# A down-projection in Strassen form with seven quadrant products, its shared sums carried on by copying PSUM banks

## The chip, the cores and the metric

One Trainium2 chip, one core. The metric is the device time of one launch in microseconds (us). The kernel before takes 472.49 us (median of 4 runs, 472.24 to 472.75). Batches are numbered from 0 to 7. A "half" is half of one batch's sequence, 512 positions. The engines are called by the profile's names: PE multiplies matrices, PEld loads its weights, DVE and ACT work on elements, POOL issues the k, v, q and weight loads, SP issues the transposing transfers. PSUM is the memory in which PE adds up its products; a bank is one tile of it, here 128x512 in fp32. The "granted clock" is PE's clock in the profile, as a share of full speed.

## The reference

Linear attention with a fixed projection, then a token-and-channel mixer, over 8 batches of 1024 positions:

```python
k_proj = einsum('ks,bhsd->bhkd', E, k);  v_proj = einsum('ks,bhsd->bhkd', F, v)   # 64 of 1024
attn   = softmax(q @ k_proj.T / 8);      x = heads_side_by_side(attn @ v_proj)    # (8, 1024, 512)
u  = x + (relu(x.T @ w_tok1) @ w_tok2).T          # token mixing
out = u + relu(u @ w_ch1) @ w_ch2                 # channel mixing, 512 -> 1536 -> 512
```

The last product, `relu(...) @ w_ch2`, is the down-projection that the change rewrites.

## The kernel before

Everything runs in bf16 with fp32 sums in PSUM. While the "back" of batch b (channel mixing: `up` and `down`) runs, the "front" of batch b+1 (projections, attention, token mixing) is cut into small units that are put between its blocks, and the k, v and q of batch b+2 are loaded. Parts of the code:

```python
def q_transpose(b):                       # two transposing transfers, SBUF to SBUF, issued by SP
    for h in range(0, H, H // 2):
        tc.keep_in_program_order(nc.sync.dma_start_transpose(out=qT[:, h:h+H//2]..., in_=q_sb[:, h:h+H//2]...))

def ch2(i, ss, part):                     # 4 of the 12 products of one 128x512 output tile
    if part == 0:
        st["o"] = psC.tile([P, DM], F32, tag="c", name="o2_ps")
    for cc in range(part * 4, part * 4 + 4):
        nc.tensor.matmul(o2_ps, st["gT", i][:, cc, ss*P:(ss+1)*P], wc2_sb[:, cc, :], ...)
    if part == CC // 4 - 1:
        nc.vector.tensor_add(out=o_sb, in0=o2_ps, in1=u_sb[:, si, :]); stores.append(...)

def load_ahead(b, cc):                    # the loads wait for Relu tile cc of the batch's first half
    passed = nc.gpsimd.tensor_copy(out=gate, in_=first_tile()[0:1, cc, 0:1])
    with tc.issue_after(passed.ins):
        load_kv(b + 2, 2); load_q(b + 2, 2)

units = front_units(b + 1)
units.append(lambda b=b: q_transpose(b + 2))        # last unit of the batch
for n, block in enumerate(blocks):
    block()
    if b > 0 and n == 5:
        load_ahead(b, 5)
    # [...] then as many units as are due
```

"The u transpose" below is SP's other transfer, which turns u into the uT that the up-projection reads. A scheduler orders the instructions of each engine when the kernel is built, and the profile shows the engines starting them in that order: on DVE in batch 0, below, an addition that was ready stands behind an operation that waits.

The softmax here doesn't subtract the row's maximum and nothing guards it: scores larger than these inputs give would overflow.

Of the kernel before, what the change touches and what calls it, by code (L numbers as in the profile page):

```python
# [8 lines left out]
F32 = mybir.dt.float32  # L9
BF16 = mybir.dt.bfloat16  # L10
# [5 lines left out]
def kernel(  # L16
# [13 lines left out]
    nc = tc.nc  # L30
    P = 128

    B, H, S, D = q.shape
    KP = E.shape[0]
    DM = H * D
# [3 lines left out]
    NSI = S // P  # L39
    NJ = NSI // 2  # L40
    TC = DT // P
    DMC = DM // P
    CC = DC // P
    HP = H // 2
    S2 = S // 2
# [1 line left out]
    scale = 1.0 / (D ** 0.5)  # L47

    const = ctx.enter_context(tc.tile_pool(name="const", bufs=1))
    kv_pool = ctx.enter_context(tc.tile_pool(name="kv", bufs=2))  # L50
    small = ctx.enter_context(tc.tile_pool(name="small", bufs=2))
    attn_pool = ctx.enter_context(tc.tile_pool(name="attn", bufs=4))
    mix_pool = ctx.enter_context(tc.tile_pool(name="mix", bufs=2))
    gT_pool = ctx.enter_context(tc.tile_pool(name="gT", bufs=2))
    out_pool = ctx.enter_context(tc.tile_pool(name="outp", bufs=5))
    psC = ctx.enter_context(tc.tile_pool(name="psC", bufs=3, space=bass.MemoryType.PSUM))
    psA = ctx.enter_context(tc.tile_pool(name="psA", bufs=2, space=bass.MemoryType.PSUM))
    psS = ctx.enter_context(tc.tile_pool(name="psS", bufs=1, space=bass.MemoryType.PSUM))
# [11 lines left out]
    def load_kv(b, parts):  # L70
        k_sb, v_sb, q_sb = [
            kv_pool.tile([P, H, NSI, D], BF16, tag=name, name=name) for name in ("k_sb", "v_sb", "q_sb")
        ]
        qT = mix_pool.tile([P, H, NJ, P], BF16, tag="qT", name="qT")
        loaded[b] = (k_sb, v_sb, q_sb, qT)
        hn = H // parts
        for h in range(0, H, hn):
            for t, src in ((k_sb, k), (v_sb, v)):
                nc.gpsimd.dma_start(
                    out=t[:, h : h + hn],  # L80
                    in_=src[b, h : h + hn].rearrange("h (p si) d -> p h si d", p=P),
                )

    def load_q(b, parts):
        hn = H // parts
        for h in range(0, H, hn):
            nc.gpsimd.dma_start(
                out=loaded[b][2][:, h : h + hn],
                in_=q[b, h : h + hn].rearrange("h (p si) d -> p h si d", p=P),
            )  # L90

    def q_transpose(b):
        q_sb, qT = loaded[b][2:]
        for h in range(0, H, H // 2):
            tc.keep_in_program_order(
                nc.sync.dma_start_transpose(
                    out=qT[:, h : h + H // 2].rearrange("p h j s -> p (h j) s"),
                    in_=q_sb[:, h : h + H // 2].rearrange("p h si d -> p (h si d)"),
                )
            )  # L100

    load_kv(0, HP)
    load_q(0, HP)

# [5 lines left out]
    for c in range(0, DC, DC // 4):  # L110
        nc.gpsimd.dma_start(
            out=wc1_sb[:, :, c : c + DC // 4],
            in_=moe_w_ch1.rearrange("(dc p) c -> p dc c", p=P)[:, :, c : c + DC // 4],
        )
    load_kv(1, 2)
    load_q(1, 2)
    wc2_sb = const.tile([P, CC, DM], BF16, name="wc2_sb")
    for c in range(0, CC, CC // 4):
        nc.gpsimd.dma_start(
            out=wc2_sb[:, c : c + CC // 4],  # L120
            in_=moe_w_ch2.rearrange("(cc p) d -> p cc d", p=P)[:, c : c + CC // 4],
# [15 lines left out]
    for src, dst in ((E_sb, ET_sb), (F_sb, FT_sb)):  # L137
# [2 lines left out]
            nc.tensor.transpose(e_ps[:, si, :], src[:, si:S:NSI], ident[:KP, :KP])  # L140
        nc.vector.tensor_copy(out=dst, in_=e_ps)

    uTs = {}
    us = {}

    def front_units(b):

        k_sb, v_sb, q_sb, qT = loaded.pop(b)
        vb = vbs[b % 2]
        x_sb = mix_pool.tile([P, NSI, DM], BF16, tag="x_sb", name="x_sb")  # L150
        u_sb = mix_pool.tile([P, NSI, DM], BF16, tag="u_sb", name="u_sb")
        hT_sb = mix_pool.tile([P, TC, DM], BF16, tag="hT_sb", name="hT_sb")
        uT = [
            mix_pool.tile([P, NJ, DMC, P], BF16, tag=f"uT{i}", name=f"uT{i}") for i in range(2)
        ]
# [1 line left out]
        st = {}  # L157

        def q_transpose_pe(hp):
            t_ps = psC.tile([P, 2, NJ, P], BF16, tag="c", name="t_ps")  # L160
            for h in range(2):
                for j in range(NJ):
                    nc.tensor.transpose(  # L163
                        t_ps[:, h, j, :],
                        q_sb[:, 2 * hp + h, 2 * j : 2 * j + 2, :].rearrange("p s d -> p (s d)"),
                        ident,
                    )
            nc.scalar.copy(out=qT[:, 2 * hp : 2 * hp + 2], in_=t_ps)  # L168
# [117 lines left out]
        if b == 0:  # L286
            for hp in range(HP):
                kv_proj(2 * hp, 2)
                k_transpose(2 * hp, 2)
            q_transpose_pe(0)  # L290
            q_transpose_pe(1)
            scores(0)
            q_transpose_pe(2)
            scores(1)
            attend(0)
# [31 lines left out]
        units = [kv_proj, k_transpose]  # L327
# [11 lines left out]
    stores = []  # L339

    def flush(n):

        for dst, o_sb in stores[:n]:
            nc.scalar.dma_start(out=dst, in_=o_sb)
        del stores[:n]

    out_v = out.rearrange("b (p si) d -> b p si d", p=P)

    def back_blocks(b):

        u_sb, uT = us.pop(b), uTs.pop(b)
        st = {}

        def ch1(i, cc):
            g_ps = psC.tile([P, S2], F32, tag="c", name="g_ps")
            for dc in range(DMC):
                nc.tensor.matmul(  # L357
                    g_ps, wc1_sb[:, dc, cc * P : (cc + 1) * P], uT[i][:, :, dc, :],
                    start=(dc == 0), stop=(dc == DMC - 1),
                )  # L360
            nc.scalar.activation(out=st["gT", i][:, cc, :], in_=g_ps, func=ACT.Relu)  # L361

        def ch2(i, ss, part):
            if part == 0:
                st["o"] = psC.tile([P, DM], F32, tag="c", name="o2_ps")
            o2_ps = st["o"]
            for cc in range(part * 4, part * 4 + 4):
                nc.tensor.matmul(  # L368
                    o2_ps, st["gT", i][:, cc, ss * P : (ss + 1) * P], wc2_sb[:, cc, :],
                    start=(cc == 0), stop=(cc == CC - 1),  # L370
                )
            if part == CC // 4 - 1:
                si = i * NJ + ss
                o_sb = out_pool.tile([P, DM], F32, tag="o_sb", name="o_sb")
                nc.vector.tensor_add(out=o_sb, in0=o2_ps, in1=u_sb[:, si, :])  # L375
                stores.append((out_v[b, :, si, :], o_sb))

        def half(i):
            st["gT", i] = gT_pool.tile([P, CC, S2], BF16, tag="gT", name="gT")

        up, down = [], []
        for i in range(2):
            up.append([lambda i=i: (half(i), ch1(i, 0))])
            up[i] += [lambda i=i, cc=cc: ch1(i, cc) for cc in range(1, CC)]
            down.append(
                [lambda i=i, ss=ss, p=p: ch2(i, ss, p) for ss in range(NJ) for p in range(CC // 4)]
            )
        if b == 0:
            blocks = up[0] + up[1] + down[0] + down[1]
        else:  # L390
            blocks = up[0] + down[0] + up[1] + down[1]
        return blocks, lambda: st["gT", 0]
# [3 lines left out]
    def load_ahead(b, cc):  # L396

        if b + 2 < B:
            passed = nc.gpsimd.tensor_copy(out=gate, in_=first_tile()[0:1, cc, 0:1])  # L399
            with tc.issue_after(passed.ins):  # L400
                load_kv(b + 2, 2)
                load_q(b + 2, 2)

    rest = front_units(0)
    for b in range(B):
        blocks, first_tile = back_blocks(b)
        if b == 0:
            for n, block in enumerate(blocks[:16]):
                block()
                if rest:  # L410
                    rest.pop(0)()
            load_ahead(0, 0)
            blocks = blocks[16:]
        n0, n1 = (0, len(blocks) - 4) if b == 0 else (2, len(blocks) - 4)
        units = front_units(b + 1) if b + 1 < B else []
        if b + 2 < B:
            units.append(lambda b=b: q_transpose(b + 2))
        done = 0
        for n, block in enumerate(blocks):
            made = len(stores)  # L420
            block()
            if b > 0 and n == 5:
                load_ahead(b, 5)
            want = max(0, n + 1 - n0) * len(units) // (n1 - n0)
            while done < min(want, len(units)):
                units[done]()
                done += 1
            flush(made)
# [29 lines left out]
```

## Time and profile before

| stage | from, to (us) | length |
|---|---|---|
| batch 0, with its own front | 0 to 98.6 | 98.6 |
| batches 1 to 6, each | for example 153.1 to 207.6 | 54.5 |
| batch 7, nothing beside it | 425.6 to 471.2 | 45.6 |

A stage ends, to 0.2 us, where the next batch's first up-projection matmul starts. First the page's busy times of the kernel before, as a share of the span:

```profile
PE 451.5 (96%) x2588; PEld 221.8 (47%) x2624; DVE 175.0 (37%) x345; ACT 165.0 (35%) x259; POOL 50.1 (11%) x78
```

Then its table by stretches. After the stretch and its length come the busy us of each engine, the clock granted to PE, the share of the DMA engines and GB/s:

```profile
0.00:98.60 98.60, 84.71 (x653) 50.10 (x658) 41.60 (x102) 37.15 (x55) 26.95 (x43) 1.00 0.95 165
153.10:207.60 54.50, 54.24 (x293) 25.48 (x296) 21.16 (x39) 18.93 (x30) 4.64 (x7) 1.00 0.70 136
425.60:471.20 45.60, 41.37 (x191) 18.60 (x190) 6.23 (x9) 14.27 (x24) 0.00 (x0) 1.00 0.18 63
```

In a middle batch PE is busy 54.24 of 54.50 us at full clock. It waits for nothing, so a microsecond of PE issue saved should be a microsecond gained, and a new wait of PE should cost its whole length.

### The profile page before, as it was taken

How to read it: one execution, taken by the hardware profiler on the slowest of the kernel's cores; microseconds unless marked ns; L12 is line 12 of the kernel's file. 1: busy time of each engine (PE TensorE's matmuls, PEld its weight loads, DVE VectorE, ACT ScalarE, POOL GpSimd, SP SyncE). 2: the span in 40 equal slices, each digit the busy share in tenths (PEclk: the TensorE clock that was granted, in tenths of full speed). 3: DMA queues.
4: the chain of work that ended last, by engine and by line, in shares of the span. 5: the costliest groups of instructions: out<-in, count | busy, mean ns of one | idle time of the engine just before them, and what ended most of it. 6: DMA issues, size and time to landing. Idle time of an engine off the chain costs nothing.

```text
span 471.2 us, 6248 instructions
## 1 busy us (share of the span) xinstructions
PE 451.5 (96%) x2588; PEld 221.8 (47%) x2624; DVE 175.0 (37%) x345; ACT 165.0 (35%) x259; POOL 50.1 (11%) x78
## 2 busy tenths in 40 slices
PE   2789999999999999999999999999999999999996
PEld 2567455444544444444444445443444445444442
DVE  3454026533524343423614425242524236150202
ACT  1256581026250533316151352406242162505060
POOL 8532300003000210003000030003000000000000
PEclk9999999999999999999999999999999999999999
DMA  8999993389905895279913898069942812033102
GB/s 118 208 203 207 206 206 105 84 188 164 212 1 130 162 206 131 48 170 145 222 41 90 178 165 193 1 159 155 207 106 67 176 26 90 0 90 89 68 22 89
DMA packets 93051, 60.43 MB, mean 128 GB/s; under 512 B 56160, under 2 KB 84320, under 8 KB 93024
## 3 DMA queue, kind: packets, MB, share of 16 engines
q0 software_dynamic: 29728, 29.63, 38.6%
q1 hardware_dynamic: 54080, 13.63, 16.7%
q10 hardware_dynamic: 9216, 16.78, 9.9%
q8 instruction: 20, 0.33, 0.3%
q14 instruction: 7, 0.06, 0.0%
HBM read 59.24 MB, written 16.78 MB: 161 GB/s over the span
## 4 chain that ended last, share of the span: by engine, by line
PE 93%; DMA 4%; DVE 1%; POOL 1%; issue 1%; POOLq 0%
PE g_ps L357 36%; PE o_ps L368 35%; PE u_ps L243 5%; PE h_ps L234 5%; PE o_ps L216 3%; PE kv_ps L178 3%; PE s_ps L204 2%; DMA q_sb<-in_q_dram 2%; DMA k_sb<-in_k_dram 1%; PE up_ps L271 1%; PE t_ps L163 1%; PE hp_ps L260 1%; DVE x_sb L224 1%; PE kt_ps L193 1%; PE ut_ps L281 0%
## 5 line engine op out<-in xcount | busy, mean ns | idle before, releaser
L361 ACT ACTIVATE gT<-g_ps 128x512 bf16<-128x512 f32 x192 | 114.9, 601 | 216.8 <-PE g_ps L357 194.8
L368 PE MATMUL o_ps<-wc_sb,gT 128*128 128x512 bf16 x744 | 180.7, 379 | 1.4
L357 PEld LDWEIGHTS <-wc_sb 128*128 128x128 bf16 x768 | 71.7, 98 | 84.4 <-issue 7.2
L368 PEld LDWEIGHTS <-gT 128*128 128x128 bf16 x768 | 72.5, 98 | 78.4 <-issue 2.0
L375 DVE TENSOR_TENSOR o_sb<-o_ps,u_sb 128x512 f32<-128x512 f32 x64 | 44.3, 691 | 77.3 <-PE o_ps L368 77.3
L247 DVE TENSOR_TENSOR u_sb<-u_ps,x_sb 128x512 bf16<-128x512 f32 x56 | 38.7, 691 | 91.5 <-PE u_ps L243 84.0
L224 DVE TENSOR_TENSOR x_sb<-o_ps,rdn 128x512 bf16<-128x512 f32 x64 | 44.3, 692 | 2.2
L209 ACT ACTIVATE a_sb<-s_ps 128x1024 bf16<-128x1024 f32 x32 | 33.0, 1033 | 28.2 <-PE s_ps L204 28.2
L223 DVE RECIPROCAL rdn<-o_ps 128x8 f32<-128x8 f32 x64 | 13.0, 204 | 64.5 <-PE o_ps L216 64.4
L243 PE MATMUL u_ps<-hT_sb,wt_sb 128*128 128x512 bf16 x107 | 32.2, 378 | 0.1
L183 DVE CAST kp_sb<-kv_ps 64x512 bf16<-64x512 f32 (+1 forms) x22 | 10.9, 532 | 48.0 <-PE kv_ps L179 48.0
L216 PEld LDWEIGHTS <-a_sb 128*128 128x128 bf16 x256 | 20.2, 101 | 15.9 <-DVE x_sb L224 2.7
L399 POOL COPY gate<-gT 1x1 bf16<-1x1 bf16 x6 | 1.1, 178 | 248.1 <-ACT gT L361 248.1
L234 PE MATMUL h_ps<-x_sb,wt_sb 128*128 128x512 bf16 x105 | 26.1, 379 | 0.4
L243 PEld LDWEIGHTS <-wt_sb 128*128 128x128 bf16 x112 | 16.1, 144 | 12.2 <-issue 2.6
L179 PE MATMUL kv_ps<-v_sb,FT_sb 128*64 128x512 bf16 (+1 forms) x88 | 17.4, 354 | 4.0 <-DMA v_sb<-in_v_dram 4.0
L178 PE MATMUL kv_ps<-k_sb,ET_sb 128*64 128x512 bf16 (+1 forms) x88 | 18.3, 355 | 1.9 <-DMA k_sb<-in_k_dram 1.9
L234 PEld LDWEIGHTS <-wt_sb 128*128 128x128 bf16 x112 | 10.9, 98 | 13.2
L238 ACT ACTIVATE hT_sb<-h_ps 128x512 bf16<-128x512 f32 x14 | 8.4, 598 | 24.1 <-PE h_ps L234 24.1
L216 PE MATMUL o_ps<-vb_134,a_sb 128*128 128x130 bf16 x128 | 13.7, 235 | 1.8 <-DVE x_sb L224 1.8
L178 PEld LDWEIGHTS <-ET_sb 128*64 128x64 bf16 x88 | 8.9, 129 | 12.5 <-issue 7.7
L168 ACT COPY qT<-t_ps 128x1024 bf16<-128x1024 bf16 x8 | 8.2, 1030 | 18.1 <-PE t_ps L163 18.1
(67 smaller groups left out, 356.2 us busy)
## 6 DMA issues: line engine op xcount, KB each, us to landing
out_dram<-o_sb ACTq DMA_DIRECT2D x64, 256.0 KB, 3.5
k_sb<-in_k_dram POOLq DMA_DIRECT2D x14, 512.0 KB, 9.2
v_sb<-in_v_dram POOLq DMA_DIRECT2D x14, 512.0 KB, 11.8
q_sb<-in_q_dram POOLq DMA_DIRECT2D x14, 512.0 KB, 17.5
wc_sb<-in_moe_w_ch_dram POOLq DMA_DIRECT2D x8, 384.0 KB, 16.8
k_sb<-in_k_dram POOLq DMA_DIRECT2D x4, 256.0 KB, 7.3
v_sb<-in_v_dram POOLq DMA_DIRECT2D x4, 256.0 KB, 7.9
q_sb<-in_q_dram POOLq DMA_DIRECT2D x4, 256.0 KB, 10.0
```

The source lines that it names most:

```text
L178: nc.tensor.matmul(kv_ps[0:KP], ET_sb[:, si, :], k_sb[:, hs, si, :], start=a, stop=z)
L179: nc.tensor.matmul(kv_ps[KP : 2 * KP], FT_sb[:, si, :], v_sb[:, hs, si, :], start=a, stop=z)
L209: nc.scalar.activation(out=a_sb, in_=s_ps, func=ACT.Exp, scale=scale)
L216: nc.tensor.matmul(o_ps[:, j // 2, (j % 2) * 2 * D1 : (j % 2 + 1) * 2 * D1], a_sb[:, h % 2, j * P : (j + 1) * P], vb[:, h // 2, h % 2].rea ...
L224: nc.vector.tensor_tensor(out=x_sb[:, :, h * D : (h + 1) * D].rearrange("p (n c) d -> p n c d", n=2), in0=o4[:, :, :, 0:D], in1=rdn[:, :, ...
L234: nc.tensor.matmul(h_ps, wt1_sb[:, si, t * P : (t + 1) * P], x_sb[:, si, :], start=(si == 0), stop=(si == NSI - 1),)
L243: nc.tensor.matmul(u_ps, wt2_sb[:, t, si::NSI], hT_sb[:, t, :], start=(t == 0), stop=(t == TC - 1),)
L247: nc.vector.tensor_add(out=u_sb[:, si, :], in0=u_ps, in1=x_sb[:, si, :])
L357: nc.tensor.matmul(g_ps, wc1_sb[:, dc, cc * P : (cc + 1) * P], uT[i][:, :, dc, :], start=(dc == 0), stop=(dc == DMC - 1),)
L361: nc.scalar.activation(out=st["gT", i][:, cc, :], in_=g_ps, func=ACT.Relu)
L368: nc.tensor.matmul(o2_ps, st["gT", i][:, cc, ss * P : (ss + 1) * P], wc2_sb[:, cc, :], start=(cc == 0), stop=(cc == CC - 1),)
L375: nc.vector.tensor_add(out=o_sb, in0=o2_ps, in1=u_sb[:, si, :])
```

## The change

The intent: a 2x2 block product by Strassen (in Winograd's arrangement) needs 7 products of quadrants instead of 8. Per half, the 12 chunks of the inner dimension, the 512 output columns and the 512 positions are each cut in two. 48 matmuls of 512 columns become 7 x 12 = 84 of 256 columns. The weight side has its four sums made once, the activation side four sums per half on DVE. The outputs share partial sums. The change gets these by letting PE accumulate in bank A, copying A to B on ACT, and going on accumulating in both. To make room, k, v, q, qT, x and h go from two buffers to one. The diff, cut to its core (the comments are not in the code, and the lines p1 to p4 sum up the seven products; left out are fewer output buffers, three larger ones instead of five, and another PSUM pool for the q transposes that PE makes in batch 1):

```diff
-    kv_pool = ctx.enter_context(tc.tile_pool(name="kv", bufs=2))
+    kv_pool = ctx.enter_context(tc.tile_pool(name="kv", bufs=1))
-        qT = mix_pool.tile([P, H, NJ, P], BF16, tag="qT", name="qT")
+        qT = one_pool.tile([P, H, NJ, P], BF16, tag="qT", name="qT")      # [...] x_sb, hT_sb too
+    def weight_sums():                      # T[0] = B12-B11, T[1] = B22-T[0], T[2] = B22-B12, T[3] = B21-T[1]
+        nc.vector.tensor_sub(out=T[0], in0=B12, in1=B11)                  # [...]
+        def act_sums(i, c0, c1):            # for two chunks at a time
+            nc.vector.tensor_add(out=S1, in0=A21, in1=A22)
+            nc.vector.tensor_sub(out=S2_, in0=S1, in1=A11)
+            nc.vector.tensor_sub(out=S3, in0=A11, in1=A21)
+            nc.vector.tensor_sub(out=S4, in0=A12, in1=S2_)
+        def product(bank, left, right, first, last):
+            for t in range(2):
+                for cc in range(CH):
+                    nc.tensor.matmul(bank[:, t, :], left[:, cc, t*P:(t+1)*P], right[:, cc, :],
+                        start=(first and t == 0 and cc == 0), stop=(last and cc == CH - 1), ...)
+        def fork(src, dst):
+            nc.scalar.copy(out=bank(dst), in_=st[src])
+            # p1: A  = A11 B11, fork A->B     p5: E = S1 T0 (other bank)   p6: B += S2 T1, fork B->C
+            # p2: A += A12 B21, out 11        p7: C += S3 T2, fork C->D, out 22 (with E)
+            # p3: B += S4 B22, out 12 (with E)                 p4: D += A22 T3, out 21
             load_ahead(0, 0)
+            weight_sums()
-            if b > 0 and n == 5:
-                load_ahead(b, 5)
+            if b > 0 and n == 5:
+                load_ahead(b, 2)            # the chunks now run 0, 6, 1, 7, 2, ...: chunk 2 is the fifth Relu
+        t0, t1 = (0, total - 8) if b == 0 else (4, total - 8)             # units are due by cost, up to t1
-            while done < min(want, len(units)):
+            while free and done < min(want, len(units)):
```

The stores become 32 of 512 KB instead of 64 of 256 KB.

More of the change, by code (lines that the diff above doesn't have):

```diff
@@ L53 @@
     mix_pool = ctx.enter_context(tc.tile_pool(name="mix", bufs=2))
+    one_pool = ctx.enter_context(tc.tile_pool(name="one", bufs=1))
     gT_pool = ctx.enter_context(tc.tile_pool(name="gT", bufs=2))
-    out_pool = ctx.enter_context(tc.tile_pool(name="outp", bufs=5))
+    out_pool = ctx.enter_context(tc.tile_pool(name="outp", bufs=3))
     psC = ctx.enter_context(tc.tile_pool(name="psC", bufs=3, space=bass.MemoryType.PSUM))
@@ L141 @@
         nc.vector.tensor_copy(out=dst, in_=e_ps)
+    CH, DH = CC // 2, DM // 2
+    B11, B12 = wc2_sb[:, 0:CH, 0:DH], wc2_sb[:, 0:CH, DH:DM]
+    B21, B22 = wc2_sb[:, CH:CC, 0:DH], wc2_sb[:, CH:CC, DH:DM]
+    tw_sb = const.tile([P, 4, CH, DH], BF16, name="tw_sb")
+    def weight_sums():
+        T = [tw_sb[:, n] for n in range(4)]
+        nc.vector.tensor_sub(out=T[0], in0=B12, in1=B11)
+        nc.vector.tensor_sub(out=T[1], in0=B22, in1=T[0])
+        nc.vector.tensor_sub(out=T[2], in0=B22, in1=B12)
+        nc.vector.tensor_sub(out=T[3], in0=B21, in1=T[1])
     uTs = {}
@@ L149, in front_units @@
         vb = vbs[b % 2]
-        x_sb = mix_pool.tile([P, NSI, DM], BF16, tag="x_sb", name="x_sb")
+        x_sb = one_pool.tile([P, NSI, DM], BF16, tag="x_sb", name="x_sb")
         u_sb = mix_pool.tile([P, NSI, DM], BF16, tag="u_sb", name="u_sb")
-        hT_sb = mix_pool.tile([P, TC, DM], BF16, tag="hT_sb", name="hT_sb")
+        hT_sb = one_pool.tile([P, TC, DM], BF16, tag="hT_sb", name="hT_sb")
         uT = [
@@ L159, in q_transpose_pe @@
         def q_transpose_pe(hp):
-            t_ps = psC.tile([P, 2, NJ, P], BF16, tag="c", name="t_ps")
+            pool, tag = (psC, "c") if b == 0 else (psA, "a")
+            t_ps = pool.tile([P, 2, NJ, P], BF16, tag=tag, name="t_ps")
             for h in range(2):
@@ L361, in ch1 @@
             nc.scalar.activation(out=st["gT", i][:, cc, :], in_=g_ps, func=ACT.Relu)
-        def ch2(i, ss, part):
-            if part == 0:
-                st["o"] = psC.tile([P, DM], F32, tag="c", name="o2_ps")
-            o2_ps = st["o"]
-            for cc in range(part * 4, part * 4 + 4):
-                nc.tensor.matmul(
-                    o2_ps, st["gT", i][:, cc, ss * P : (ss + 1) * P], wc2_sb[:, cc, :],
-                    start=(cc == 0), stop=(cc == CC - 1),
-                )
-            if part == CC // 4 - 1:
-                si = i * NJ + ss
-                o_sb = out_pool.tile([P, DM], F32, tag="o_sb", name="o_sb")
-                nc.vector.tensor_add(out=o_sb, in0=o2_ps, in1=u_sb[:, si, :])
-                stores.append((out_v[b, :, si, :], o_sb))
@@ L378, in half @@
-        def half(i):
-            st["gT", i] = gT_pool.tile([P, CC, S2], BF16, tag="gT", name="gT")
-        up, down = [], []
-        for i in range(2):
-            up.append([lambda i=i: (half(i), ch1(i, 0))])
-            up[i] += [lambda i=i, cc=cc: ch1(i, cc) for cc in range(1, CC)]
-            down.append(
-                [lambda i=i, ss=ss, p=p: ch2(i, ss, p) for ss in range(NJ) for p in range(CC // 4)]
-            )
+        TH = S2 // 2
+        def act_sums(i, c0, c1):
+            g, S_ = st["gT", i], st["S", i]
+            A11, A12 = g[:, c0:c1, 0:TH], g[:, CH + c0 : CH + c1, 0:TH]
+            A21, A22 = g[:, c0:c1, TH:S2], g[:, CH + c0 : CH + c1, TH:S2]
+            S1, S2_, S3, S4 = [S_[:, n, c0:c1] for n in range(4)]
+            nc.vector.tensor_add(out=S1, in0=A21, in1=A22)
+            nc.vector.tensor_sub(out=S2_, in0=S1, in1=A11)
+            nc.vector.tensor_sub(out=S3, in0=A11, in1=A21)
+            nc.vector.tensor_sub(out=S4, in0=A12, in1=S2_)
@@ new lines, in product, with bank @@
+        def product(bank, left, right, first, last):
+            for t in range(2):
+                for cc in range(CH):
+                    nc.tensor.matmul(
+                        bank[:, t, :], left[:, cc, t * P : (t + 1) * P], right[:, cc, :],
+                        start=(first and t == 0 and cc == 0), stop=(last and cc == CH - 1),
+                        skip_group_check=True,
+                    )
+        def bank(name, pool=psC, tag="c"):
+            st[name] = pool.tile([P, 2, DH], F32, tag=tag, name=name)
+            return st[name]
@@ new lines, in fork, with down_blocks, put, p1 @@
+        def fork(src, dst):
+            nc.scalar.copy(out=bank(dst), in_=st[src])
+        def down_blocks(i):
+            r0, r1 = i * NJ, i * NJ + 2
+            U = lambda r, c: u_sb[:, r : r + 2, c * DH : (c + 1) * DH]
+            g = lambda: st["gT", i]
+            S_ = lambda n: st["S", i][:, n]
+            T = [tw_sb[:, n] for n in range(4)]
+            def put(r, c, src, other):
+                key = ("o", i, r)
+                if key not in st:
+                    st[key] = [out_pool.tile([P, 2, DM], F32, tag="o_sb", name="o_sb"), 0]
+                o_sb = st[key][0]
+                nc.vector.tensor_add(out=o_sb[:, :, c * DH : (c + 1) * DH], in0=st[src], in1=other)
+                st[key][1] += 1
+                if st[key][1] == 2:
+                    stores.append((out_v[b, :, r : r + 2, :], o_sb))
+            def p1():
+                product(bank("A"), g()[:, 0:CH, 0:TH], B11, True, False)
+                fork("A", "B")
+            def p5():
+                product(bank("E", psS, "s"), S_(0), T[0], True, True)
+                for n, r in enumerate((r0, r1)):
+                    st["e", n] = one_pool.tile([P, 2, DH], F32, tag=f"e{n}", name=f"e{n}")
+                    nc.vector.tensor_add(out=st["e", n], in0=st["E"], in1=U(r, 1))
+            def p6():
+                product(st["B"], S_(1), T[1], False, False)
+                fork("B", "C")
+            def p2():
+                product(st["A"], g()[:, CH:CC, 0:TH], B21, False, True)
+                put(r0, 0, "A", U(r0, 0))
+            def p7():
+                product(st["C"], S_(2), T[2], False, True)
+                fork("C", "D")
+                put(r1, 1, "C", st["e", 1])
+            def p3():
+                product(st["B"], S_(3), B22, False, True)
+                put(r0, 1, "B", st["e", 0])
+            def p4():
+                product(st["D"], g()[:, CH:CC, TH:S2], T[3], False, True)
+                put(r1, 0, "D", U(r1, 0))
+            return [(p1, 3, True), (p5, 3, False), (p6, 3, False), (p2, 3, True), (p7, 3, True), (p3, 3, True), (p4, 3, True)]
@@ new lines, in up_blocks, with block @@
+        def up_blocks(i):
+            def block(n):
+                if n == 0:
+                    st["gT", i] = gT_pool.tile([P, CC, S2], BF16, tag="gT", name="gT")
+                    st["S", i] = one_pool.tile([P, 4, CH, TH], BF16, tag="S", name="S")
+                ch1(i, n // 2 + CH * (n % 2))
+                if n % 4 == 3:
+                    act_sums(i, n // 2 - 1, n // 2 + 1)
+            return [(lambda n=n: block(n), 2, True) for n in range(CC)]
+        up, down = [up_blocks(0), up_blocks(1)], [down_blocks(0), down_blocks(1)]
@@ L407 @@
         if b == 0:
-            for n, block in enumerate(blocks[:16]):
+            for n, (block, cost, _) in enumerate(blocks[:16]):
                 block()
@@ L412 @@
             load_ahead(0, 0)
+            weight_sums()
             blocks = blocks[16:]
-        n0, n1 = (0, len(blocks) - 4) if b == 0 else (2, len(blocks) - 4)
         units = front_units(b + 1) if b + 1 < B else []
@@ L417 @@
             units.append(lambda b=b: q_transpose(b + 2))
-        done = 0
-        for n, block in enumerate(blocks):
+        total = sum(cost for _, cost, _ in blocks)
+        t0, t1 = (0, total - 8) if b == 0 else (4, total - 8)
+        done = t = 0
+        for n, (block, cost, free) in enumerate(blocks):
             made = len(stores)
             block()
+            t += cost
             if b > 0 and n == 5:
-                load_ahead(b, 5)
-            want = max(0, n + 1 - n0) * len(units) // (n1 - n0)
-            while done < min(want, len(units)):
+                load_ahead(b, 2)
+            want = max(0, t - t0) * len(units) // (t1 - t0)
+            while free and done < min(want, len(units)):
                 units[done]()
```

## The prediction

> **What bounds the kernel now.** The page gives PE busy 451.5 of 471.2 us; the chain that ended last is 93% PE. In the windows table each of the six middle batches takes 54.50 us with PE busy 54.2: PE issue is the limit there, with no slack. A 512-column matmul issues every 216 ns (four in 0.86 us in the chain of waits); a 128-column one, each with its own weight load, every 56 ns (sixteen in 0.89 us). Both fit columns/2.4 GHz plus about 2.5 ns, the spacing that the Trainium skill gives ("TensorE: Matmul & The Clock Gate", "Back-to-back issue gap"). So 256 columns should cost about 109 ns, weight loads hidden.
>
> **What the change removes.** Per half batch, 48 matmuls of 216 ns (10.36 us) become 84 of 109 ns (9.2 us): 1.2 us saved, 19 us over 16 halves. All of it is PE issue, on the chain.
>
> **What it adds.** ACT: 3 bank copies per half, about 0.6 us each like the 128x512 Relu (0.60). DVE: 12 bf16 sums of 512 elements per half, estimated 0.38 to 0.43 us each (the 128x512 bf16 copy took 0.425), 6 final additions of 0.69 us in place of 4, and 4 weight sums of about 0.95 us once. DVE rises from 175 to about 270 us, ACT from 165 to about 195. Neither is full, but both feed PE.
>
> **Steady batches.** Adding durations along the queue orders: most copies hide behind the product placed between copy and use (1.3 us against 0.9). The last S1 sum holds the E product about 0.4 us, and attention tiles, token-mixing tiles and the E bank, which share few banks with a fuller DVE, cost some 0.9 us more. Net gain about 1.1 us per middle batch instead of 2.4.
>
> **Batch 0, the decisive part.** In the queue order the first weight sum stands on DVE before the last attention-stage residual addition of batch 0. It waits for the first two down-projection weight loads. In the trace before, the first of these is issued at 34.7 us, and they take 17.5 to 18.8 us to land: the second lands near 55.6. PE reaches the transpose that needs that addition at 45.7 us. So PE should stand from about 45.8 until 55.6 + 0.95 + 0.4 + 0.69 = about 57.7: 12 us lost. After such a gap PE restarts cold (the skill, same page, "The HAM clock gate": idle windows of about 3.4 us bring the half-rate clock; the trace before shows 130 ns transposes at 21 us against 56 ns later): 1.5 us more. The single S buffer makes the second half's 12 sums run as a burst when the first half's products end: about 3 us. Token-mixing tiles crowded at batch 0's end, on one bank, and the transpose after them: 2.5 us.
>
> Sum: batch 0 +12 +1.5 +3 +2.5 +0.8 -2.4 = +17.4; six middle batches -6.6; the last -2.4, but its final store is 512 KB instead of 256, +1.3. Total +9.7 on 472.45: about **482.5 us, range 470 to 492**. Faster by over 2%: 5%; within 2%: 43%; slower by over 2%: 52%.
>
> **What would show it.** (1) Timeline: PE idle 46 to 57 us, released by the DVE addition, DVE waiting on the weight DMA. (2) Groups: products at about 109 ns each. (3) Windows: middle batches near 53.4 us. (4) Waits: PE waits for DVE (S1 into E; the banks) over ACT. (5) The last batch about 2 us shorter before its tail.
>
> **What would make it wrong.** The weight loads land earlier, so that the first gap shrinks (down to 467); or middle batches wait more than I added up, from DVE bursts held in order (up to 495); or 256-column products cost more than 109 ns.

## More of the kernel before

```profile
161.03 0.18 POOL L399 COPY gate<-gT 1x1 bf16<-1x1 bf16 x1 [49.53 <-ACT gT L361]
161.54 0.75 POOL L79 DMA_DIRECT2D k_sb<-in_k_dram  x1 [0.34 <-issue]
```

Around one batch boundary (batch 2 starts at 153.0), the two q transposes occupy SP from 151.72 to 159.4; the loads start at 161.54. From the first q transpose to the first load there are 9.8 us, and the issue of the pair takes 7.7 of them. That leaves 2.1 us.

Columns: start, length of the issue, engine and line, what goes where:

```profile
149.60 1.95 SPq L250 DMA_TRANSPOSE uT_1132<-u_sb  x1
151.72 7.71 SPq L96 DMA_TRANSPOSE qT<-q_sb  x2
```

## The result and the profile after

The changed kernel takes 543.53 us (median of 4 runs, 542.95 to 546.33). The ratio to before is 1.1515 (95% interval 1.1474 to 1.1557). Ratios here are the mean time of one kernel's fast runs over that of the other's of the same rounds, so they are not quite the ratio of the medians quoted. The predicted range ended at 492.

The page after, first its busy line. PE has almost the same busy sum as before (452.8 against 451.5), although it has fewer columns to stream: in several stages its granted clock is lower (0.90, in the table below):

```profile
PE 452.8 (83%) x3200; PEld 280.4 (51%) x3200; DVE 270.7 (50%) x573; ACT 193.6 (36%) x307; POOL 50.3 (9%) x78
```

The table by stretches, cut at the same events as before:

```profile
0.00:120.70 120.70, 86.53 (x742) 57.22 (x742) 58.20 (x140) 40.38 (x61) 26.88 (x43) 0.91 0.80 138
120.70:175.70 55.00, 54.19 (x357) 32.71 (x358) 30.08 (x61) 22.43 (x36) 4.88 (x7) 0.95 0.61 115
175.70:243.40 67.70, 54.82 (x370) 33.05 (x368) 32.72 (x67) 22.60 (x36) 4.64 (x7) 0.90 0.58 109
243.40:311.60 68.20, 56.48 (x370) 33.36 (x369) 32.72 (x67) 22.91 (x36) 4.64 (x7) 0.90 0.62 109
311.60:380.40 68.80, 54.43 (x370) 32.86 (x369) 32.72 (x67) 22.60 (x36) 4.63 (x7) 0.90 0.59 108
380.40:448.30 67.90, 54.87 (x371) 33.09 (x370) 32.72 (x67) 22.58 (x36) 4.62 (x7) 0.90 0.57 109
448.30:500.60 52.30, 52.28 (x369) 32.41 (x367) 32.54 (x67) 22.36 (x36) 0.00 (x0) 1.00 0.33 82
500.60:544.60 44.00, 39.20 (x266) 25.71 (x263) 18.96 (x37) 17.75 (x30) 0.00 (x0) 0.98 0.25 83
```

Against before, the stages differ by +22.1, +0.5, +13.2, +13.7, +14.3, +13.4, -2.2 and -1.6 us, in sum the 73.4 us between the two spans. So two things cost most: batch 0, and batches 2 to 5. (Batch 1 took 2.7 us more than batch 6, because PE starts it at half clock: granted 0.50 from 120.8 to 126.3, after the wait that ends batch 0.) Batch 6, for which nothing more is loaded, shows what the change does by itself: 52.3 us, with PE busy in all of it. The waits of PE, longest first (us in total, times, longest):

```profile
PE s_ps L219 <- DMA qT<-q_sb: 52.6, 8, 13.1
PE ut_ps L296 <- DVE u_sb L291: 11.5, 1, 11.5
...
PE g_ps L372 <- DMA uT_754<-u_sb: 3.7, 1, 3.7
...
PE kv_ps L193 <- DVE x_sb L239: 2.3, 1, 2.3
```

**Batch 0.** DVE's part of the timeline shows the predicted jam, then PE's part:

```profile
41.93 0.69 DVE L291 TENSOR_TENSOR u_sb<-up_ps,x_sb 128x512 bf16<-128x512 f32 x1 [0.89 <-PE up_ps L286]
54.99 0.96 DVE L152 TENSOR_TENSOR tw_sb<-wc_sb 128x1536 bf16<-128x1536 bf16 x1 [12.37 <-DMA wc_sb<-in_moe_w_ch_dram]
55.87 0.42 DVE L388 TENSOR_TENSOR S<-gT 128x512 bf16<-128x512 bf16 x1
56.21 0.68 DVE L291 TENSOR_TENSOR u_sb<-up_ps,x_sb 128x512 bf16<-128x512 f32 x1
```

```profile
44.41 1.03 PE L372 MATMUL g_ps<-uT_176,wc_sb 128*128 128x512 bf16 x4
56.95 0.61 PE L296 MATMUL ut_ps<-ident,u_sb 128*128 128x128 bf16 x4 [11.51 <-DVE u_sb L291]
57.35 8.25 PE L372 MATMUL g_ps<-uT_176,wc_sb 128*128 128x512 bf16 x28
```

The first weight sum waits 12.4 us for the weights, with an addition queued behind it that was ready long before, and PE stands 11.5 us. The 28 matmuls after that take 8.25 us, where 28 x 0.216 + 0.16 = 6.2 us would do (0.16 is what the last one outlasts its issue step): the restart at a lower clock (granted 0.50 from 57.3 to 61.4) costs 2 us.

**Batches 2 to 5.** SP's part and POOL's part of the timeline around the start of batch 2 at 175.7, to be held against those of before:

```profile
174.70 2.62 SPq L265 DMA_TRANSPOSE uT_1246<-u_sb  x1
177.50 12.84 SPq L97 DMA_TRANSPOSE qT<-q_sb  x2
```

```profile
182.64 0.18 POOL L480 COPY gate<-gT 1x1 bf16<-1x1 bf16 x1 [44.61 <-ACT gT L376]
183.18 0.74 POOL L80 DMA_DIRECT2D k_sb<-in_k_dram  x1 [0.36 <-issue]
```

The first q transpose is now issued 1.8 us after the boundary (before: 1.2 us ahead of it), and the first load 7.5 us after it (before: 8.6). Between the two lie 5.7 us instead of 9.8, too few for the 7.7 us that the pair took before. The pair also takes longer now: the issue of the first transpose alone lasts 6.1 us (5.7 to 6.4 in the four batches, 3.9 before), nearly all of it before the first load. In batch 1 of the same profile, where no store runs beside it, it lasts 2.5 us; here two stores of 512 KB do, but no run moved the stores, so that they are the cause is not shown. In all, the second transpose, which had been issued 5.9 us ahead of the first load, is issued at 183.6, 0.4 us behind it. The chain of work that ended last gives its time to land:

```profile
183.61 16.81 DMA qT<-q_sb
200.42 0.04 issue
200.46 0.64 PE s_ps L219 x3
```

It took 16.8 us; the median of all q transposes before was 6.0 and the longest 8.5. PE's part of the timeline:

```profile
187.10 1.04 PE L372 MATMUL g_ps<-uT_1245,wc_sb 128*128 128x512 bf16 x4
200.46 0.64 PE L219 MATMUL s_ps<-qT,kT 64*64 64x512 bf16 x4 [12.32 <-DMA qT<-q_sb]
201.03 3.60 PE L372 MATMUL g_ps<-uT_1245,wc_sb 128*128 128x512 bf16 x8
```

PE stands 12.3 us and starts again at half speed (8 matmuls in 3.6 us, where 1.9 us is usual). This is the pattern of every one of the four batches: the waits of PE for qT in them are 12.9, 11.7, 14.4 and 13.0 us.

Why the transposes come later: they stand behind the last token-mixing tile and the u transpose on SP. In the timeline the last token-mixing matmuls start at 148.21, 4.75 us before the next batch's first matmul at 152.96; after the change at 173.16, 2.5 us before 175.66. Units may now be put only at the blocks marked free, and they are spread by cost and no longer by number; the order that results places them nearer to the boundary. Which of the two does it was not tested.

### The profile page after: what moved, and what is told of

The parts are those of the page before. It is cut to its first block, busy times and chain, and to the rows that moved or that the text cites. A ratio compares the mean times of both kernels' runs of the same rounds, so it can differ in the third digit from the quotient of the medians.

```text
span 544.6 us, 7657 instructions
## 1 busy us (share of the span) xinstructions
PE 452.8 (83%) x3200; PEld 280.4 (51%) x3200; DVE 270.7 (50%) x573; ACT 193.6 (36%) x307; POOL 50.3 (9%) x78
## 4 chain that ended last, share of the span: by engine, by line
PE 70%; DMA 25%; DVE 2%; ACT 1%; issue 0%; POOL 0%; SPq 0%; POOLq 0%; DVEq 0%
PE g_ps L372 28%; DMA qT<-q_sb 14%; PE B L394 7%; PE A L394 7%; DMA wc_sb<-in_moe_w_ch_dram 6%; PE u_ps L258 5%; PE h_ps L249 4%; PE E L394 4%; PE C L394 4%; PE D L394 3%; PE o_ps L231 3%; PE kv_ps L193 2%; DMA q_sb<-in_q_dram 2%; DMA uT_754<-u_sb 1%; PE s_ps L219 1%; DMA v_sb<-in_v_dram 1%
## 5 line engine op out<-in xcount | busy, mean ns | idle before, releaser
L394 PEld LDWEIGHTS <-S 128*128 128x128 bf16 x768 | 73.5, 98 | 12.8 <-issue 1.1
L388 DVE TENSOR_TENSOR S<-gT 128x512 bf16<-128x512 bf16 x48 | 20.2, 421 | 109.9 <-ACT gT L376 109.9
L394 PEld LDWEIGHTS <-gT 128*128 128x128 bf16 x576 | 55.9, 98 | 8.8 <-issue 0.2
L219 PE MATMUL s_ps<-qT,kT 64*64 64x512 bf16 x128 | 14.7, 449 | 52.9 <-DMA qT<-q_sb 52.6
L394 PE MATMUL A<-wc_sb,gT 128*128 128x256 bf16 x384 | 47.5, 273 | 0.0
L386 DVE TENSOR_TENSOR S<-gT 128x512 bf16<-128x512 bf16 x48 | 20.3, 422 | 22.1 <-ACT gT L376 22.1
L394 PE MATMUL C<-tw_sb,S 128*128 128x256 bf16 x192 | 25.7, 273 | 0.0
L394 PE MATMUL B<-wc_sb,S 128*128 128x256 bf16 x192 | 25.0, 273 | 0.0
L394 PE MATMUL B<-tw_sb,S 128*128 128x256 bf16 x192 | 24.6, 273 | 0.0
L394 PE MATMUL D<-tw_sb,gT 128*128 128x256 bf16 x192 | 24.1, 273 | 0.0
L394 PE MATMUL E<-tw_sb,S 128*128 128x256 bf16 x192 | 23.6, 273 | 0.0
```

What stands on the lines that cost most here:

```text
L219: nc.tensor.matmul(s_ps[dst * KP : (dst + 1) * KP, h % 2, :], kT[rows, h, :], qT[rows, h].rearrange("p j s -> p (j s)"), start=True, stop= ...
L386: nc.vector.tensor_add(out=S1, in0=A21, in1=A22)
L394: nc.tensor.matmul(bank[:, t, :], left[:, cc, t * P : (t + 1) * P], right[:, cc, :], start=(first and t == 0 and cc == 0), stop=(last and ...
```

## The experiments

Theory 1 (collision): the q transposes and the loads of k and v meet on the DMA engines, because the change took the margin from both sides. Rival 2: the single qT and q_sb buffers hold the transposes back. Rival 3: the fuller DVE (32.7 instead of 21.2 us per batch) slows the transfers. Separately, batch 0 is the jam behind the weight sums. All ten runs gave correct results, and all times below are medians of 4 to 6 runs, slow ones included, beside the kernel before on the same chip (472.0 to 472.3 us).

### Later loads

```diff
-            if b > 0 and n == 5:
-                load_ahead(b, 2)
+            if b > 0 and n == 11:
+                load_ahead(b, 11)
```

> The changed kernel, but from batch 1 on the k, v and q loads for the batch after next are let go by the last Relu of the first up-projection half (about 13 us after the batch starts) instead of by its fifth. Theory 1 (collision): in batches 2 to 5 the second q transpose takes 17 us because the k and v loads start in the same microsecond; with the loads later the transposes take under 9 us, the PE's 12 us wait for qT goes, batches 2 to 5 fall from 68 us to about 52.5, and the total from 543.5 to about 480 (475 to 490). Rival 2 (the single qT and q_sb buffers hold the transposes back) and rival 3 (the fuller DVE slows the transfers): nothing that they name is changed, so 535 to 545.

Measured: 486.89 us, ratio 1.0314 (1.0289 to 1.0339). The waits of PE for qT in this run:

```profile
PE s_ps L219 <- DMA qT<-q_sb: 1.8, 4, 0.7
```

52.6 us of waits have become 1.8, and 56.6 us of time are gone with them, with one buffer and a full DVE as before. This is Theory 1's number; the rivals said 535 or more.

### Earlier loads in the kernel before

```diff
-            if b > 0 and n == 5:
-                load_ahead(b, 5)
+            if b > 0 and n == 0:
+                load_ahead(b, 0)
```

> The kernel before, but from batch 1 on its k, v and q loads are let go by the first Relu of the batch (about 2 us after its start) instead of by the sixth (8.4 us). Its buffers stay double and its DVE load light. Theory 1: the second q transpose of each batch now collides with the loads, takes 10 us or more instead of 6 to 8, and the PE waits for qT 3 to 6 us in most of batches 2 to 6: total 485 to 505. Rivals 2 and 3: 472 as before, since it has two buffers and no bf16 sums on DVE.

Measured: 536.65 us, ratio 1.1348 (1.1312 to 1.1384). The old kernel, without a single Strassen product, with two buffers, loses 65 us by this one line. Its waits of PE for qT, and one of them in PE's part of the timeline:

```profile
PE s_ps L204 <- DMA qT<-q_sb: 56.1, 6, 12.4
```

```profile
178.41 1.90 PE L357 MATMUL g_ps<-uT,wc_sb 128*128 128x512 bf16 x8
191.01 0.64 PE L204 MATMUL s_ps<-qT,kT 64*64 64x512 bf16 x4 [10.70 <-DMA qT<-q_sb]
```

Rivals 2 and 3 fall as the explanation: neither is present here. The size was missed: 3 to 6 us a batch and 485 to 505 us in all were expected, 56.1 us in 6 waits were measured. The second q transpose of batches 1 to 5 took 20.0 to 22.4 us to land.

### Which half of the lost margin

```diff
-                load_ahead(b, 2)
+                load_ahead(b, 8)      # the sixth Relu, as in the kernel before; it was the fifth
```

> The changed kernel with the loads let go by the sixth Relu of the batch, as in the kernel before, instead of the fifth (0.9 us later). It tells which half of the lost margin matters. If the later q transposes alone (about 3 us later against the boundary than before) are enough for the collision, it stays at 510 or more. If the one Relu by which the change moved the loads forward was the cause, it falls to about 490.

Measured: 512.52 us, ratio 1.0837 (1.0803 to 1.0872). By the letter this is the first reading, 510 or more; but moving the loads by one Relu brings back 31.0 of the 56.6 us, and the other 25.6 remain.

```profile
PE s_ps L219 <- DMA qT<-q_sb: 20.1, 7, 5.3
```

Around the start of batch 2 in this run, POOL's first load, and the second q transpose in the chain that ended last:

```profile
183.78 0.74 POOL L80 DMA_DIRECT2D k_sb<-in_k_dram  x1 [0.36 <-PE g_ps L372]
183.37 9.74 DMA qT<-q_sb
```

Much of the difference goes with the order of two issues. Here, in batches 2 to 5, the second transpose is issued 0.4 to 0.9 us ahead of the first load and takes 8.2 to 9.9 us to land. In the changed kernel it is issued with the load or up to 0.7 us behind it and takes 16.8 to 18.7, and in the old kernel with early loads, 0.2 to 2.2 us behind it, 20.0 to 22.4. Both halves of the lost margin mattered: with the loads back in their old place, the later transposes still cost 25.6 us.

### The other side moved: units that end earlier, and q transposes ahead of token mixing

```diff
-        t0, t1 = (0, total - 8) if b == 0 else (4, total - 8)
+        t0, t1 = (0, total - 8) if b == 0 else (4, total - 16)
```

> The changed kernel with its loads untouched, but from batch 1 on the next batch's units are spread to end 16 instead of 8 cost steps before the end of the batch, so that token mixing, the u transpose and the q transposes end some 5 us earlier. Theory 1: the transposes are through before the loads come, so 480 to 492 as with the late loads. If the loads are at fault for another reason than their meeting the transposes, it stays above 530.

Measured: 491.05 us, ratio of the fast runs 1.0366 (1.0318 to 1.0413); one of the four runs, the profiled one, was slow (the median of the other three is 490.38). Its profile has no wait for qT in batches 2 to 6; 9.2 us of them are left in batch 1, at whose start the transposes are those that batch 0 issues, which the edit leaves alone. A second way to the same end:

```diff
-            units.append(lambda b=b: q_transpose(b + 2))
+            units.insert(len(units) - (0 if b == 0 else 10), lambda b=b: q_transpose(b + 2))
```

> The changed kernel, but from batch 1 on the q transposes for the batch after next are issued before that batch's token mixing instead of after all of it; the loads and the single buffers stay. Theory 1: the transposes now end before the boundary, so the loads meet nothing; the PE's long waits for qT go in batches 3 to 6 (batch 2's transposes are issued in batch 0 and stay), and the total is 478 to 500. Rival 2 (single buffers): an earlier issue can only wait longer for the readers of the one buffer, so no gain: 540 or more. Rival 3: a DVE as full as before slows them as much, 530 or more.

Measured: 490.28 us, ratio 1.0373 (1.0329 to 1.0418). In this run no wait for qT is left among PE's waits. In both the loads stay where the change had put them, and only the transposes move, with the units in the first of the two. Loads later, units earlier, transposes earlier: three edits that have in common that they set the transposes and the loads apart give 487 to 491 us.

### Batch 0: the weight sums

```diff
             load_ahead(0, 0)
-            weight_sums()
+                if b == 0 and done == 2:                  # after the k transpose unit of batch 1 [...]
+                    with tc.issue_after(kt_copy[1].ins):  # behind its copy on DVE
+                        weight_sums()
```

> The changed kernel, but the four weight sums are queued on DVE behind the kT copy of batch 1 instead of ahead of batch 0's last residual addition. All theories of the middle batches leave them alone. The prediction's step for batch 0: the PE gap from 45.4 to 57.0 us and the cold restart after it go, batch 1 starts near 107 us instead of 120.7, total 543.5 to 530 (527 to 533). If the gap had another cause, batch 0 stays at 120 us.

Measured: 531.02 us, ratio of the fast runs 1.1207 (1.1144 to 1.127); one of four runs was slow (the median of the other three is 530.82). That is 12.5 us less than the changed kernel, and the wait of the u transpose for DVE is no longer among PE's waits. A first attempt, in which the sums were only called later in the program, was built and not run: the scheduler put the first of them on DVE at the same place, ahead of the addition. The ordering edge moved it.

### Repairs together

```diff
+            (the later loads and the later weight sums of above)
```

> The two repairs together: loads let go by the last Relu of the first half, weight sums behind the kT copy. If the two losses are separate, their gains add: 486.9 minus the 13 us that batch 0 gave gives 473.5 (470 to 477), still no better than the kernel before at 472.1. If they share a cause, less than 13 us more is gained.

Measured: 471.23 us, ratio 0.9998 (0.9967 to 1.0029). The two losses are separate: one edit alone gave 56.6 us and the other 12.5, together they give 72.3, some 3 us more than the sum. The changed kernel is then level with the one before.

```diff
-                    st["S", i] = one_pool.tile([P, 4, CH, TH], BF16, tag="S", name="S")
+                    st["S", i] = mix_pool.tile([P, 4, CH, TH], BF16, tag="S", name="S")
-        t0, t1 = (0, total - 8) if b == 0 else (4, total - 8)
+        t0, t1 = (0, total - 20) if b == 0 else (4, total - 8)
```

> The same, with two buffers for the S sums (12 KB more per partition) and batch 0's next-batch units spread to end 20 instead of 8 cost steps before its end. The prediction's two small steps for batch 0: the burst of sums held the PE 2.3 us (wait of the k/v projection for DVE), and the crowded token-mixing tiles with the transpose behind them 5.3 us plus a cold restart. Both should go: 466 (461 to 470), faster than before by over 1%. If those waits only move elsewhere, 473.

Measured: 463.63 us, ratio 0.9841 (0.9808 to 0.9874): faster by 1.6%. The wait of the k/v projection for DVE (2.3 us) and that of the up-projection for the u transpose (3.7 us) are gone from PE's waits. The two edits were not run apart. What was left was 4.6 us of waits for qT:

```diff
-        t0, t1 = (0, total - 20) if b == 0 else (4, total - 8)
+        t0, t1 = (0, total - 20) if b == 0 else (4, total - 14)
```

> The repaired version (late loads, late weight sums, two S buffers, batch 0 spread), with the middle batches' units also ended 14 instead of 8 cost steps before the end. In the profile of the repaired version the PE still waits 4.6 us for qT in the middle batches. Theory 1: with the q transposes some 4 us earlier these go, and the middle batches come to about 52 us: 459 (456 to 463). If what is left is not the collision, 463 to 464 as without it.

Measured: 459.88 us (458.80 to 460.63), ratio 0.9733 (0.9709 to 0.9756): faster than the kernel before by 2.7%. Two middle batches in its table by stretches:

```profile
151.90:204.30 52.40, 52.19 (x367) 32.22 (x368) 32.60 (x67) 22.19 (x36) 4.82 (x7) 1.00 0.76 141
204.30:256.70 52.40, 52.19 (x367) 32.24 (x368) 32.59 (x67) 22.18 (x36) 4.82 (x7) 1.00 0.77 141
```

PE is busy in all of 52.4 us again, now 2.1 us less than before. No wait for qT is left in its list.

Instead of that last edit, the q transposes ahead of token mixing (the same line as above):

> The repaired version (late loads, late weight sums, two S buffers, batch 0 spread), with the q transposes from batch 1 on issued ahead of the token mixing. Theory 1: the same 4.6 us of qT waits go by the other road, 459 (456 to 463). If the transposes only meet another transfer there (the stores of the first half), 463 or more.

Measured: 462.62 us, ratio 0.9799 (0.9772 to 0.9826), which is unclear against the 2%. This is at the upper end of what was expected, but the reason is not the transposes: no wait for qT is left among PE's waits here either. A middle batch is longer than in the run before, with PE busy in nearly all of it:

```profile
203.80:257.00 53.20, 52.93 (x367) 32.38 (x369) 32.40 (x67) 22.39 (x36) 4.82 (x7) 1.00 0.71 139
```

What the 0.8 us more per batch are was not followed up.

## Why the prediction was wrong, point by point

- **PE issue (right).** A product of twelve 256-column matmuls takes 1.31 us in the chain, 109 ns each, weight loads hidden, as predicted. The saving is 2 x (48 x 0.216 - 84 x 0.109) = 2.4 us per batch; PE's busy time fell by 2.05 (54.24 to 52.19, in the run that is left without waits for qT).
- **Copies and sums (right in size).** ACT copies took 0.57 to 0.58 us each, the bf16 sums 0.42, DVE rose to 270.7 us and ACT to 193.6.
- **Waits of a middle batch on DVE and ACT (too pessimistic).** I added up 1.3 us per batch. Batch 6, which meets no loads, ran 52.3 us with PE busy 52.28: there were none. "Net gain about 1.1 us per middle batch" was 2.2 there.
- **The step that failed: the sum for the middle batches has no term for the transfers.** "Steady batches" adds up PE, ACT and DVE; SP and POOL do not occur in it, and its six middle batches came to -6.6 us. In fact the first q transpose moved 3.1 us later against the boundary, its issue grew by 2.2 us, and the loads moved 1.1 us earlier. The second transpose then landed in 16.8 to 18.7 us, and four batches lost 13 to 14 us each, 54.6 us in all. The runs show it from both kernels: later loads take the loss away from the changed one, earlier loads bring it about in the old one. The two moves and the margin of 2.1 us could have been read from the diff, the queue orders and the trace before; nothing in the prediction asks what the loads run beside.
- **Batch 0 (right in mechanism, somewhat short in size).** Predicted +17.4, measured +22.1. The gap was 11.5 us (12 predicted) from 45.4 to 57 (45.8 to 57.7), the cold restart after it 2 us (1.5), the burst of sums 2.3 (3). The end of batch 0 was mis-sized: three short waits of token mixing for DVE, together 1.7 us, then 3.7 us for the u transpose, make 5.4 us where I had 2.5. The restart at half clock after that falls into batch 1 and is most of what batch 1 lost. The late weight sums alone gave back 12.5 us (15.7 once the loads were repaired).
- **Cold restarts (right).** The Trainium skill ("TensorE: Matmul & The Clock Gate", "Part 1: The HAM clock gate") says that a pause of a few microseconds brings PE back to half clock. The trace agrees: after 12.3 us of standing, 8 matmuls took 3.6 us, where 1.9 us is usual.
- **The last batch (right).** -1.6 us where -1.1 was predicted.

How the DMA engines share their time between a transpose and a load can be read from the packets in the trace. The Trainium skill ("DMA: Bandwidth & Descriptors", "Issuing engines are not separate DMA queues") says that transfers from all issuers run on the same 16 engines and interleave, and ("Queues, rings and completion order") that an engine takes turns between rings packet by packet. The packets that the profile records agree with that: there are as many of one kind as of the other. First the changed kernel from 190 to 199 us, with the loads (q0) and the second transpose (q1) in flight, then the run with late loads from 183 to 186 us, with the transpose alone. Columns: packets, MB, and the time that the packets took as a share of 16 engines' time (packets overlap, so it can pass 100%):

```profile
q0 software_dynamic: 1399, 1.40, 91.4%
q1 hardware_dynamic: 1396, 0.36, 30.5%
```

```profile
q1 hardware_dynamic: 2837, 0.72, 119.8%
```

Beside the loads it is one packet for one, and a load's packet carries 1.0 KB where a transpose's carries 0.26. The transpose falls from 946 packets a microsecond to 155, while the loads keep most of their pace (155 packets a microsecond, against 185 in the kernel before from 166 to 176 us).

What stays open is the part of the 512 KB stores, which are issued at 175.3 and 176.9, right beside the u transpose: that one took 9.2 us to land, 4.8 before. With the stores in place and the loads out of the way, in batch 6 and in the run with late loads, PE lost next to nothing (none in batch 6, 1.8 us in the whole run). So the stores alone are not the loss, but they may have helped to push the second transpose behind the first load.

## What to carry to other kernels

An engine that is off the critical path still has a timetable, and a tuned kernel may depend on a margin in it that no busy share shows: before changing the order of work, list the transfers around each stage boundary with their order and their distances, and check both after. Where a waiting instruction is queued ahead of a ready one on an engine that works in order, the wait is passed on to everybody behind it, so an operation on late data belongs behind the ready work; here its place in the program did not put it there, and an explicit ordering edge did. And before a change that costs time is given up, take its side effects away one by one: here the same arithmetic was 15% slower as it came and 2.7% faster than the old kernel after four small edits to its schedule and one more buffer.

## What the Trainium skill lacked or had wrong

- "DMA: Bandwidth & Descriptors", "Rules for kernel authors", says that a DMA transpose next to ordinary DMAs needs nothing. For correctness the runs agree. For time they do not: beside four k and v loads a q transpose took 16.8 us to land in the changed kernel, against a median of 6.0 in the kernel before, and up to 22.4 us in the old kernel with early loads. No page gives a size for this, or says that taking turns by packet puts the transfer with the smaller packets at a disadvantage (0.26 KB against 1.0 KB here).
- "TensorE: Matmul & The Clock Gate", "Back-to-back issue gap", gives about 81 ns (128 columns) and 131 ns (512 columns) per matmul for a real stream of weight load and matmul pairs. Such pairs ran at 56, 109 and 216 ns for 128, 256 and 512 columns, which is the formula that the page calls isolated.
- "PSUM — Partial Sum Buffer", "The four PSUM rules", advises that a sum seeded by an engine must start from 0 to be safe either way. Here banks filled by an ACT copy (128x512 fp32, 0.57 us) were accumulated into by PE, and all nine runs of variants of the changed kernel were correct. The page's own rule for banks whose bits earlier matmuls left set would explain it; no run here reads those bits. The copied bank as a way to share partial sums is not described.
